# Attention read-out and soft mixture of experts on one core: a ring of 21 buffers of 8 KB per partition in place of 43 of 4 KB

## The chip, the core and the metric

The kernel runs on one core of one Trainium2 chip. What counts is the device time of one execution in microseconds (us). The kernel before took 134.65 us, the median of 3 runs (134.57 to 135.22). The core has five engines with a queue of instructions each: TensorE (PE, with its weight loads listed as PEld), VectorE (DVE), ScalarE (ACT), GpSimd (POOL) and SyncE (SP). Transfers between HBM and the on-chip memory SBUF are issued by an engine's queue (here SP's, and twice ACT's) and carried out by 16 DMA engines. SBUF has 128 partitions; a transfer of a tile moves one row per partition. All data is float32. In sizes, 1 MB is 1,048,576 bytes and 1 KB is 1,024.

## The reference

Eight batches b, eight heads, 512 tokens of width 64 and 32 states per head. First an attention in both directions between tokens and states, then a soft mixture of 8 experts with 4 slots each over all 4608 rows:

```python
scores = scale * x @ state.T;      a  = softmax(scores);   xread = a  @ state
scores2 = scale * state @ x.T;     a2 = softmax(scores2);  sread = a2 @ x
x = concat([xread, sread], tokens)            # (4608, 512)
logits = x @ phi                              # 32 slots
d = softmax(logits, over rows)
slot_input = d.T @ x                          # (32, 512), needs every row
h = relu(slot_input[e] @ w1[e])               # per expert e, w1[e] 512 x 1024
slot_out[e] = h @ w2[e]                       # w2[e] 1024 x 512
out = softmax(logits, over slots) @ slot_out  # (4608, 512)
```

The inputs x and the two weights are 8 MB, 16 MB (w1) and 16 MB (w2). The output is 8.5 MB. No weight can be used before the slot inputs are known, and these need every row of the attention.

## The kernel before, in words

**Stages.** The attention stage runs over the batches; the order of its small steps on all engines is written out in the table `ORDER`, and no scheduler changes it. In it `X.b.g` (L204) transposes a quarter g of batch b on PE, and `R.b.h` (L311) is the last step that reads x of batch b. The stage ends with `SI` (L594), which gives the slot inputs. The h stage (L640) multiplies them with w1: for each half hf of the hidden width and each expert e four column blocks, which together use 1 MB of w1. The so stage (L700) multiplies with w2, for a quarter k of the output width, a half hf and an expert e. `out(k, q)` makes 1 MB of output: eight matmuls into four PSUM tiles (L730), two copies by ACT (L739) and two by DVE (L740) into buffers, and transfers to HBM (L741). `out_st(k)` makes the small output for the state rows, sent in two transfers (L759). The so stage of the next k is interleaved with the outputs of the last.

**The buffer ring.** x, the weights, the outputs and the transposed states `stT_sb` share one pool `big` of `NBIG` = 43 buffers of 4 KB per partition (0.5 MB each). Tiles take the buffers in turn: the n-th tile takes the buffer of the one 43 before it and can be filled once that has been used for the last time. First come `stT_sb` (one buffer) and x (two buffers per batch), then weights are loaded ahead into the 26 buffers that are left. Later loads are issued where the code has freed buffers: two after `R.b.1` (so 16 over the stage), one after the last use of `stT_sb`, and two after each expert of the h stage (`load_w` in `w1_part`). Thus 43 weight buffers are loaded before the first expert of the h stage has been computed; the rest follow as the h stage frees its buffers.

**The queue.** All these transfers stand on SP's queue in program order. The framework gives each transfer one of eight semaphores in rotation (DMAHW0 to DMAHW7 in the listings), and the issue of a transfer waits for the one eight before it to have landed. So at most eight transfers are in flight. An `[waits ...]` in a listing names the semaphores that the instruction waits for: those of DMA, of PE, DVE and ACT (Activation); the number after the underscore has no meaning here.

Of the kernel before, what the change touches and what calls it, by code (L numbers as in the profile page):

```python
# [8 lines left out]
F32 = mybir.dt.float32  # L9
# [6 lines left out]
P = 128  # L16
B = 8
# [7 lines left out]
NBIG = 43  # L25
# [39 lines left out]
def attention_soft_moe(ctx: ExitStack, tc: tile.TileContext, x, stT, phi, w1, w2, out_x, out_s):  # L65
# [14 lines left out]
    stT_sb = big.tile([P, 4, 2, 2, 2, NS], F32, tag="big", name="stT_sb")  # L80
    phi_sb = cp.tile([P, 4, NS], F32, name="phi_sb")
    xb = []
    for b in range(B):
        for k in range(2):
            t = big.tile([P, 2, NJ, 2 * D], F32, tag="big", name=f"x{b}_{k}")
            xv = x[b].rearrange("p (g j c) -> p g j c", g=4, j=NJ)
            if b == 0:
                for g, eng in enumerate((nc.sync, act)):
                    eng.dma_start(t[:, g], xv[:, 2 * k + g])
            else:  # L90
                nc.sync.dma_start(t, xv[:, 2 * k : 2 * k + 2])
            xb.append(t)
# [11 lines left out]
    def load_w2(t, k, e, ft):  # L104
        n = t.shape[1] // P
        t = t.rearrange("p (k f) -> p k f", k=n)
        nc.sync.dma_start(t, w2[e, k, :, ft : ft + n, :])
        for i in range(n):
            w2t[k, e, ft + i] = t[:, i]

    def load_w(n):
        for _ in range(min(n, len(todo))):
            layer, hf, e, k = todo.pop(0)
            t = big.tile([P, F], F32, tag="big", name=f"w{layer}_{hf}_{e}_{k}")
            if layer == 1:
                t = t.rearrange("p (k f) -> p k f", k=2)
                nc.sync.dma_start(t, w1[hf, e, :, 2 * k : 2 * k + 2, :])
                for i in range(2):
                    w1t[hf, e, 2 * k + i] = t[:, i]
            else:  # L120
                load_w2(t, hf, e, k)
# [33 lines left out]
    with ExitStack() as actx:  # L155
# [44 lines left out]
        def X(b, g):  # L200
            r = R[b]
            r[f"xp{g}"] = p = ps_t.tile([P, S], F32, tag="tr", name=f"xt_ps{b}_{g}")
            for j in range(NJ):
                pe.transpose(p[:, P * j : P * j + P], xb[2 * b + g // 2][:, g % 2, j, :], ident)  # L204
# [100 lines left out]
        def R_(b, h):  # L305
# [3 lines left out]
            for j in range(NJ):  # L309
                for g in range(4):  # L310
# [3 lines left out]
                        xb[2 * b + g // 2][:, g % 2, j, D * h : D * h + D],  # L314
# [3 lines left out]
            if h == 1:  # L318
                load_w(2)
# [301 lines left out]
        load_w(NBIG - 2 * B - 1)  # L621
        order = ORDER.split()

        last = max(order.index(f"S.{B - 1}"), order.index("U.1"))
        for i, step in enumerate(order):
# [210 lines left out]
```

## Time and profile before

One profiled execution spans 133.9 us; the runs had a median of 134.65 us, so about 0.75 us lie outside the span.

| What | Value |
|---|---|
| moved by DMA | 51.76 MB (decimal), mean 387 GB/s over the span |
| PE, DVE, ACT, POOL busy | 116.5, 86.0, 79.3, 44.8 us |
| weight transfers | 64 of 512 KB, median 10.0 us from issue to landing |
| output transfers of x rows | 16 of 512 KB, median 5.5 us from issue to landing |
| DMA queue of SP | 14544 packets, 50.93 MB (decimal) |

A row of a table by windows gives the window and its length in us, then the busy time and, in brackets, the instructions of PE, PEld, DVE, ACT and POOL, then the granted clock of PE as a share of full speed, the mean busy share of the 16 DMA engines (which can be a little over 1 because packets overlap) and the GB/s that they moved. A row of a timeline gives the start, the time, the engine (SPq is SP's queue), the line, the operation, output and input, and the count. A row of waits gives who waited for whom, the total in us, how often, and the longest.

### The profile page before, as it was taken

How to read it: one execution, taken by the hardware profiler on the slowest of the kernel's cores; microseconds unless marked ns; L12 is line 12 of the kernel's file. 1: busy time of each engine (PE TensorE's matmuls, PEld its weight loads, DVE VectorE, ACT ScalarE, POOL GpSimd, SP SyncE). 2: the span in 40 equal slices, each digit the busy share in tenths (PEclk: the TensorE clock that was granted, in tenths of full speed). 3: DMA queues.
4: the chain of work that ended last, by engine and by line, in shares of the span. 5: the costliest groups of instructions: out<-in, count | busy, mean ns of one | idle time of the engine just before them, and what ended most of it. 6: DMA issues, size and time to landing. Idle time of an engine off the chain costs nothing.

```text
span 133.9 us, 5045 instructions
## 1 busy us (share of the span) xinstructions
PE 116.5 (87%) x2103; PEld 81.5 (61%) x2103; DVE 86.0 (64%) x216; ACT 79.3 (59%) x195; POOL 44.8 (33%) x64
## 2 busy tenths in 40 slices
PE   0698999999999999999799959999999899999700
PEld 0647676868786867667667636763597449394200
DVE  2009999999999999999995377008940352333610
ACT  3068999999999989888967702210101362535700
POOL 3005383473849066078885247001600000000000
PEclk9999999999999999999999986999999999999995
DMA  3999999999999999999999984999999999998994
GB/s 88 307 391 423 416 415 424 410 421 405 419 415 416 420 413 421 416 419 413 421 410 424 405 345 153 377 399 419 415 420 413 424 410 419 413 418 330 420 415 169
DMA packets 14854, 51.76 MB, mean 387 GB/s; under 512 B 1648, under 2 KB 1904, under 8 KB 14832
## 3 DMA queue, kind: packets, MB, share of 16 engines
q1 hardware_dynamic: 14544, 50.93, 94.8%
q10 hardware_dynamic: 288, 0.52, 1.1%
q8 instruction: 16, 0.26, 0.7%
q14 instruction: 6, 0.05, 0.1%
HBM read 42.53 MB, written 8.91 MB: 384 GB/s over the span
## 4 chain that ended last, share of the span: by engine, by line
PE 45%; DVE 37%; ACT 5%; issue 4%; DMA 3%; DVEq 1%; ACTq 0%
PE h_ps L640 12%; PE so_ps L700 11%; PE o L730 7%; DVE aT L261 6%; DVE l1s L247 6%; DVE q L231 6%; DVE m L236 5%; DVE nm L267 5%; PE xt_ps L204 5%; DMA x<-x_in 3%; DVE r L252 3%; PE sc L218 2%; PE eT_ps L286 2%; PE os L748 2%; ACT out L739 1%
## 5 line engine op out<-in xcount | busy, mean ns | idle before, releaser
L204 PE MATMUL xt_ps<-ident,x 128*128 128x128 f32 x128 | 19.5, 294 | 4.6 <-DMA x<-x_in 4.6
L240 POOL TENSOR_TENSOR q<-q,m 128x512 f32<-128x512 f32 x16 | 16.7, 1049 | 16.7 <-DVE m L236 7.0
L740 DVE COPY out<-o 128x512 f32<-128x512 f32 x16 | 10.3, 686 | 18.7 <-PE o L730 18.7
L209 ACT ACTIVATE xt<-xt_ps 128x512 f32<-128x512 f32 x32 | 18.9, 618 | 5.7 <-PE xt_ps L204 5.6
L204 PEld LDWEIGHTS xt_ps<-ident,x 128*128 128x128 f32 x128 | 15.5, 151 | 7.2 <-issue 5.4
L256 POOL TENSOR_TENSOR q<-q,r 128x512 f32<-128x512 f32 x16 | 16.7, 1048 | 8.0 <-DVE r L252 2.7
L700 PEld LDWEIGHTS so_ps<-w,h_m 128*32 128x32 f32 x512 | 13.8, 110 | 4.2 <-issue 4.1
L640 PE MATMUL h_ps<-w,si_m 128*32 128x512 f32 x128 | 16.0, 650 | 0.4 <-DVE si_m L612 0.4
L700 PE MATMUL so_ps<-w,h_m 128*32 128x128 f32 x512 | 15.6, 274 | 0.8 <-issue 0.8
L231 DVE STREAM_TRANSPOSE q<-sc 128x512 f32<-128x512 f32 x16 | 11.1, 695 | 7.7 <-PE sc L218 7.7
L739 ACT COPY out<-o 128x512 f32<-128x512 f32 x16 | 8.6, 588 | 7.2 <-PE o L730 7.2
L640 PEld LDWEIGHTS h_ps<-w,si_m 128*32 128x32 f32 x128 | 8.7, 118 | 6.3 <-issue 3.6
L272 ACT ACTIVATE e<-sc,nm 128x512 f32<-128x512 f32 x16 | 11.3, 707 | 1.0 <-DVE q L231 0.4
L261 DVE STREAM_TRANSPOSE aT<-q 128x512 f32<-128x512 f32 x16 | 10.8, 687 | 0.2 <-PE eT_ps L286 0.2
L286 PE MATMUL eT_ps<-ident,e 128*128 128x128 f32 x64 | 10.2, 280 | 0.7 <-ACT e L272 0.5
L311 PE MATMUL sr_ps<-x,eT 128*32 128x64 f32 x512 | 10.3, 220 | 0.3 <-ACT eT L294 0.3
L243 ACT ACTIVATE q<-q 128x512 f32<-128x512 f32 x16 | 10.5, 658 | 0.0
L247 DVE TENSOR_REDUCE l1s<-q 128x16 f32<-128x512 f32 x16 | 10.5, 656 | 0.0
L236 DVE TENSOR_REDUCE m<-q 128x16 f32<-128x512 f32 x16 | 10.5, 659 | 0.0
L267 DVE TENSOR_REDUCE nm<-sc 128x1 f32<-128x512 f32 x16 | 10.5, 660 | 0.0
L286 PE MATMUL an_ps<-ident,aT 128*128 128x128 f32 x64 | 9.9, 280 | 0.2 <-DVE aT L261 0.2
L730 PE MATMUL o<-lt_all,so_r 32*128 32x512 f32 x64 | 9.9, 640 | 0.2 <-ACT out L739 0.2
(115 smaller groups left out, 179.3 us busy)
## 6 DMA issues: line engine op xcount, KB each, us to landing
w<-w_in SPq DMA_DIRECT2D x64, 512.0 KB, 10.0
out_x<-out SPq DMA_DIRECT2D x16, 512.0 KB, 5.5
x<-x_in SPq DMA_DIRECT2D x14, 512.0 KB, 9.3
x<-x_in ACTq DMA_DIRECT2D x2, 256.0 KB, 4.7
x<-x_in SPq DMA_DIRECT2D x2, 256.0 KB, 4.3
out_s<-out_s SPq DMA_DIRECT2D x2, 256.0 KB, 5.1
stT_sb<-stT_in SPq DMA_DIRECT2D x1, 384.0 KB, 7.5
stT_sb<-stT_in SPq DMA_DIRECT2D x1, 128.0 KB, 5.6
```

What stands on the lines that cost most here:

```text
L204: pe.transpose(p[:, P * j : P * j + P], xb[2 * b + g // 2][:, g % 2, j, :], ident)
L209: act.mul(r[f"xt{g}"], r[f"xp{g}"], 0.125)
L231: dve.transpose(r[f"q{h}"], r[f"sp{h}"])
L236: dve.tensor_reduce(out=r[f"m1{h}"], in_=r[f"qv{h}"], axis=AX.X, op=ALU.max)
L240: pool.tensor_tensor(v, v, R[b][f"m1{h}"].broadcast_to([P, 16, NS]), op=ALU.subtract)
L247: dve.tensor_reduce(out=l1s[:, i, :, 0:1], in_=R[b][f"qv{h}"], axis=AX.X, op=ALU.add)
L261: dve.transpose(r[f"aT{h}"], r[f"q{h}"])
L267: dve.tensor_reduce(out=r[f"nm2{h}"], in_=r[f"sp{h}"], axis=AX.X, op=ALU.max, negate=True)
L286: pe.transpose(p[:, j, :], r[f"{src}{h}"][:, P * j : P * j + P], ident)
L640: pe.matmul(h_ps[hf][32 * kt : 32 * kt + 32, :], si_m[kt // 2][:, 256 * (kt % 2) + 32 * e : 256 * (kt % 2) + 32 * e + 32], w1t[hf, e, kt], ...
L700: pe.matmul(so[k][32 * i : 32 * i + 32, :], h_m[hf][:, 256 * i + 32 * e : 256 * i + 32 * e + 32], w2t[k, e, 4 * hf + i], start=(hf == 0 an ...
L730: pe.matmul(o[j], so_r[hf][rows, col : col + 128], lt_all[rows, 4 * q : 4 * q + 4, :].rearrange("p b s -> p (b s)"), start=True, stop=True,)
```

## The change

The ring becomes 21 buffers of 8 KB per partition, 1 MB each. `stT_sb` leaves the ring for the pool of constants, so the memory is the same: 43 x 4 KB = 21 x 8 KB + 4 KB = 172 KB per partition. x of a batch is one tile; batches 2 to 7 come in one transfer each, batch 0 in four quarters and batch 1 in two halves as before. A w1 tile holds a whole (hf, e), a w2 tile two experts of a k, for which w2 and the output have another layout in HBM, so that rows of 8 KB are contiguous. An `out(k, q)` is one tile; for k < 3 it is sent in one transfer after all four copies, for k = 3 in two halves as before. There are 46 transfers fewer. The step that loaded into the buffer of `stT_sb` is gone.

```diff
-NBIG = 43
+NBIG = 21
-    stT_sb = big.tile([P, 4, 2, 2, 2, NS], F32, tag="big", name="stT_sb")
+    stT_sb = cp.tile([P, 4, 2, 2, 2, NS], F32, name="stT_sb")
...
+        t = big.tile([P, 4, NJ, 2 * D], F32, tag="big", name=f"x{b}")
+        if b == 0:
+            for g in range(4):
+                (act if g % 2 else nc.sync).dma_start(t[:, g], xv[:, g])
+        elif b == 1:
+            for g in (0, 2):
+                nc.sync.dma_start(t[:, g : g + 2], xv[:, g : g + 2])
+        else:
+            nc.sync.dma_start(t, xv)
...
-    todo = [(1, hf, e, k) for hf in range(2) for e in range(E) for k in range(2)]
-    todo += [(2, k, e, 0) for k in range(4) for e in range(E)]
+    todo = [(1, hf, e) for hf in range(2) for e in range(E)]
+    todo += [(2, k, e) for k in range(4) for e in range(0, E, 2)]
...
+            t = big.tile([P, 2 * F], F32, tag="big", name=f"w{layer}_{k}_{e}")
+            if layer == 1:
+                nc.sync.dma_start(t, w1[k, e])
+            else:
+                nc.sync.dma_start(t, w2[e // 2, k])
...
             if h == 1:
-                load_w(2)
+                load_w(1)
...
-        load_w(NBIG - 2 * B - 1)
+        load_w(NBIG - B)
-            if i == last:
-                load_w(1)
...
-            load_w(2)
+            load_w(1)
...
+            ot = big.tile([P, NJ, 512], F32, tag="big", name=f"out{k}_{q}")
             for jp in range(2):
-                ot = big.tile([P, 2, 512], F32, tag="big", name=f"out{k}_{q}_{jp}")
-                act.copy(ot[:, 0, :], o[2 * jp])
-                dve.tensor_copy(ot[:, 1, :], o[2 * jp + 1])
-                nc.sync.dma_start(out_x[k, q, jp].rearrange("p (i s) -> p i s", i=2), ot)
+                act.copy(ot[:, 2 * jp, :], o[2 * jp])
+                dve.tensor_copy(ot[:, 2 * jp + 1, :], o[2 * jp + 1])
+                if k == 3:
+                    two = slice(2 * jp, 2 * jp + 2)
+                    nc.sync.dma_start(out_x[k, q, :, two], ot[:, two])
+            if k < 3:
+                nc.sync.dma_start(out_x[k, q], ot)
```

Two places on SP's queue show what moves. The first is where loading ahead ends and the h stage begins to free buffers. The names there are w_k_e for w2 of quarter k and expert e, then running numbers; the tile is given as partitions by elements. Before, the loads ahead of the h stage end with w_1_2, the 43rd weight tile; w_1_3 is the first that waits for PE's h stage:

```order
L107 DMA w_0_7_0_1355<-w_in 128x1024 [waits DMAHW4_49,PE_49]
L107 DMA w_1_0_0_1501<-w_in 128x1024 [waits DMAHW5_49,PE_49]
L107 DMA w_1_1_0_1503<-w_in 128x1024 [waits DMAHW6_49,PE_49]
L107 DMA w_1_2_0_1555<-w_in 128x1024 [waits DMAHW7_49,PE_49]
L107 DMA w_1_3_0_1778<-w_in 128x1024 [waits DMAHW0_49,PE_49]
L107 DMA w_1_4_0_1780<-w_in 128x1024 [waits DMAHW1_49,PE_49]
```

In the change each name stands for two experts, and the loads ahead of the h stage end with w_1_0, the 21st weight tile:

```order
L117 DMA w_0_4_1194<-w_in 128x2048 [waits DMAHW1_49,PE_49]
L117 DMA w_0_6_1301<-w_in 128x2048 [waits DMAHW2_49,PE_49]
L117 DMA w_1_0_1447<-w_in 128x2048 [waits DMAHW3_49,PE_49]
L117 DMA w_1_2_1720<-w_in 128x2048 [waits DMAHW4_49,PE_49]
L117 DMA w_1_4_1726<-w_in 128x2048 [waits DMAHW5_49,PE_49]
```

Expert 2 of k = 1, which was among the loads ahead, is now in the first tile that waits for the h stage: 0.5 MB has moved from one side of that point to the other.

The second place is the end of the queue, the outputs of k = 2 and k = 3 (the names out_q_jp before, out_q now):

```order
L759 DMA out_s<-out_s_2099 128x512 [waits DMAHW5_49,Activation_49]
L741 DMA out_x<-out_0_0_2216 128x1024 [waits DMAHW6_49,DVE_49,Activation_49]
L741 DMA out_x<-out_0_1_2220 128x1024 [waits DMAHW7_49,DVE_49,Activation_49]
L741 DMA out_x<-out_1_0_2299 128x1024 [waits DMAHW0_49,DVE_49,Activation_49]
L741 DMA out_x<-out_1_1_2303 128x1024 [waits DMAHW1_49,DVE_49,Activation_49]
L741 DMA out_x<-out_0_0_2322 128x1024 [waits DMAHW2_49,DVE_49,Activation_49]
L741 DMA out_x<-out_0_1_2326 128x1024 [waits DMAHW3_49,DVE_49,Activation_49]
```

The same stretch in the change, where the first row is the small output of the state rows too:

```order
L758 DMA out_s<-out_s_2017 128x512 [waits DMAHW3_49,Activation_49]
L740 DMA out_x<-out_0_2130 128x2048 [waits DMAHW4_49,DVE_49,Activation_49]
L740 DMA out_x<-out_1_2211 128x2048 [waits DMAHW5_49,DVE_49,Activation_49]
L738 DMA out_x<-out_0_2232 128x1024 [waits DMAHW6_49,DVE_49,Activation_49]
L738 DMA out_x<-out_0_2232 128x1024 [waits DMAHW7_49,DVE_49,Activation_49]
```

The two halves of out(2, 1), which could each go once its two copies were made, are one transfer that waits for all four copies; those of k = 3 stay halves.

More of the change, by code (lines that the diff above doesn't have):

```diff
@@ L83, in attention_soft_moe @@
     for b in range(B):
[L84 to L92, printed above, removed]
+        t = big.tile([P, 4, NJ, 2 * D], F32, tag="big", name=f"x{b}")
+        xv = x[b].rearrange("p (g j c) -> p g j c", g=4, j=NJ)
+        if b == 0:
[6 more added lines that the diff above has]
+            nc.sync.dma_start(t, xv)
+        xb.append(t)
         if b == 0:
@@ L100, in attention_soft_moe @@
     w1t, w2t = {}, {}
-    todo = [(1, hf, e, k) for hf in range(2) for e in range(E) for k in range(2)]
-    todo += [(2, k, e, 0) for k in range(4) for e in range(E)]
[L104 to L109, printed above, removed]
+    todo = [(1, hf, e) for hf in range(2) for e in range(E)]
+    todo += [(2, k, e) for k in range(4) for e in range(0, E, 2)]
     def load_w(n):
         for _ in range(min(n, len(todo))):
-            layer, hf, e, k = todo.pop(0)
-            t = big.tile([P, F], F32, tag="big", name=f"w{layer}_{hf}_{e}_{k}")
+            layer, k, e = todo.pop(0)
+            t = big.tile([P, 2 * F], F32, tag="big", name=f"w{layer}_{k}_{e}")
             if layer == 1:
[L116 to L119, printed above, removed]
-            else:
-                load_w2(t, hf, e, k)
+                t = t.rearrange("p (k f) -> p k f", k=4)
+                nc.sync.dma_start(t, w1[k, e])
+                for i in range(4):
+                    w1t[k, e, i] = t[:, i]
+            else:
+                t = t.rearrange("p (e k f) -> p e k f", e=2, k=8)
+                nc.sync.dma_start(t, w2[e // 2, k])
+                for i in range(16):
+                    w2t[k, e + i // 8, i % 8] = t[:, i // 8, i % 8]
     def st_t(b, g):
@@ L203, in X @@
             for j in range(NJ):
-                pe.transpose(p[:, P * j : P * j + P], xb[2 * b + g // 2][:, g % 2, j, :], ident)
+                pe.transpose(p[:, P * j : P * j + P], xb[b][:, g, j, :], ident)
         def xe(b, g):
@@ L313, in R_ @@
                         r[f"eT{h}"][:, j, 32 * g : 32 * g + 32],
-                        xb[2 * b + g // 2][:, g % 2, j, D * h : D * h + D],
+                        xb[b][:, g, j, D * h : D * h + D],
                         start=(j == 0),
@@ L620, in attention_soft_moe @@
         )
-        load_w(NBIG - 2 * B - 1)
+        load_w(NBIG - B)
         order = ORDER.split()
-        last = max(order.index(f"S.{B - 1}"), order.index("U.1"))
-        for i, step in enumerate(order):
+        for step in order:
             name, *args = step.split(".")
             steps[name](*map(int, args))
-            if i == last:
-                load_w(1)
         h_ps = [ps_s.tile([P, 512], F32, tag="sc", name=f"h_ps{i}") for i in range(2)]
@@ L706, in w2_part @@
                 )
-            if hf:
+            if hf and e % 2:
                 load_w(1)
@@ L823 @@
         "w1_in": con(moe_w1.reshape(E, 4, P, 2, 512).transpose(3, 0, 2, 1, 4)),
-        "w2_in": con(moe_w2.reshape(E, 8, P, 4, P).transpose(0, 3, 2, 1, 4)),
+        "w2_in": con(moe_w2.reshape(E // 2, 2, 8, P, 4, P).transpose(0, 4, 3, 1, 2, 5)),
     }
@@ L832 @@
     r = _run(nc, [arrays], core_ids=[0]).results[0]
-    ox = r["out_x"].reshape(4, 2, 2, P, 2, 4, P).transpose(1, 5, 2, 4, 6, 0, 3).reshape(B, S, 512)
+    ox = r["out_x"].reshape(4, 2, P, 2, 2, 4, P).transpose(1, 5, 3, 4, 6, 0, 2).reshape(B, S, 512)
     os_ = r["out_s"].reshape(2, P, 2, B, NS).transpose(3, 4, 0, 2, 1).reshape(B, NS, 512)
```

2 lines of the change are left out of this document (1 added, 1 removed).

## The prediction

> **What bounds the kernel now.** I read the page first, its slices and the table of DMA issues.
>
> ```profile
> GB/s 88 307 391 423 416 415 424 410 421 405 419 415 416 420 413 421 416 419 413 421 410 424 405 345 153 377 399 419 415 420 413 424 410 419 413 418 330 420 415 169
> w<-w_in SPq DMA_DIRECT2D x64, 512.0 KB, 10.0
> ```
>
> A slice is 3.35 us. The DMA engines move about 417 GB/s from the fourth slice on, except in two holes: slices 24 to 26 and slice 37. Eight transfers of 512 KB in flight take 10.0 us at that rate (8 x 524,288 B / 417 GB/s = 10.06 us), so the queue is always full and the issue costs nothing. The table of windows shows the steady part and, in single microseconds, the holes and the end:
>
> ```profile
> 14.00:74.00 60.00, 58.18 (x1187) 43.47 (x1187) 57.28 (x150) 55.63 (x144) 33.67 (x42) 1.00 1.03 417
> 79.00:80.00 1.00, 0.69 (x4) 0.47 (x8) 0.94 (x5) 0.00 (x0) 0.00 (x0) 0.74 0.67 274
> 81.00:82.00 1.00, 1.00 (x10) 0.70 (x6) 0.96 (x2) 0.00 (x0) 1.00 (x1) 0.50 0.15 57
> 82.00:83.00 1.00, 1.00 (x11) 0.72 (x7) 0.96 (x3) 0.63 (x1) 0.71 (x2) 0.55 0.65 160
> ...
> 122.50:122.75 0.25, 0.19 (x1) 0.19 (x2) 0.25 (x2) 0.25 (x2) 0.00 (x0) 1.00 0.45 180
> 123.25:123.50 0.25, 0.25 (x5) 0.25 (x8) 0.01 (x1) 0.21 (x1) 0.00 (x0) 1.00 0.36 147
> 123.50:123.75 0.25, 0.25 (x4) 0.03 (x4) 0.00 (x0) 0.16 (x1) 0.00 (x0) 1.00 0.95 393
> 131.00:132.00 1.00, 0.00 (x0) 0.00 (x0) 0.00 (x0) 0.00 (x0) 0.00 (x0) 0.50 0.80 328
> ```
>
> In the attention stage DVE is the bound (57.28 of 60 us) and the DMA runs behind it, loading ahead. The first hole begins near 79 us, when everything that fits in the ring has landed. The waits of SP's queue from 73 us on name its end, and the timeline gives the moment:
>
> ```profile
> SPq L107 <- PE h_ps L640: 10.4, 6, 7.9
> 81.31 20.20 SPq L107 DMA_DIRECT2D w<-w_in  x21
> ```
>
> At 81.31 us the first expert of the h stage has freed its weights and SP issues again; 21 of the 64 weight transfers are left. From then on two things run side by side. The DMA has 10.5 MB of weights and 8.5 MB of output to move. PE has its own chain, which waits for no weight:
>
> ```profile
> 79.31 10.68 PE h_ps L640 x80
> 90.58 5.29 PE h_ps L640 x48
> 117.20 3.63 PE so_ps L700 x128
> 120.83 1.11 PE o L730 x8
> 121.94 0.57 ACT out L739
> ```
>
> The chain of waits from 79.31 on is almost all PE. The two meet in the second hole: at 122.5 us the DMA share falls to 0.45, to rise again at 123.5. So about half of the engines have run out of work for 1 us, because PE had not made out(2, 1), while the other half is still busy with older transfers until about 123.45. From 123.5 on all are busy until 132. The end is out(2, 1) plus what follows it: 3.25 MB, 3.41e6 B / 417 GB/s = 8.2 us.
>
> **The change part by part.** *Loading ahead.* Before, 43 x 0.5 = 21.5 MB of weights land before the hole; now 21 MB. The point at which loading resumes hangs on PE's first expert and stays at 81.31. So 0.5 MB more is to be moved after it: 524,288 B / 417 GB/s = +1.26 us of DMA work. The DMA stops 1.26 us sooner before the hole, which gives nothing back.
>
> *Issues.* 46 transfers fewer on SP's queue; with a full queue that is 0, and where SP waits for PE (81.31) one issue stands in place of two. If the cover were gone, an issue would cost the 0.33 us of its row below.
>
> *Bytes in flight.* Eight transfers are now 8 MB, and outputs still stand behind the last weights, as they did: 0.
>
> *The whole out(2, 1).* Its halves were issued as their copies ended; now one transfer waits for the last copy:
>
> ```profile
> 122.72 0.33 SPq L741 DMA_DIRECT2D out_x<-out  x1
> ...
> 123.32 0.33 SPq L741 DMA_DIRECT2D out_x<-out  x1
> ```
>
> The first row became data at 123.5, 0.8 us later. Now the issue comes at 123.32 and data at 124.1: +0.60 us for engines that have run dry. The earlier outputs, whole too, find a queue that is behind, so their later issue is covered by it; without this cover each would cost 0.6 us at the most. SP waits longer, but only outputs stand behind it, none of which is ready sooner (out(3, 0) is issued at 125.17).
>
> *The rate with rows of 8 KB.* No transfer here has such rows. The nearest rows are these, the queue of SP from 20 to 60 us (4 KB rows) and that of ACT in the first 14 us (2 KB rows), as packets, MB, share of 16 engines' time:
>
> ```profile
> q1 hardware_dynamic: 4546, 16.55, 101.7%
> ...
> q10 hardware_dynamic: 288, 0.52, 10.8%
> ```
>
> Nine packets are one transfer's part on one engine (eight rows and a completion). With 4 KB rows that part took 1.017 x 40 x 16 / (4546 / 9) = 1.29 us, with 2 KB rows 0.108 x 14 x 16 / 32 = 0.76 us. A straight line through both gives 2.35 us at 8 KB against 2 x 1.29 = 2.58: 9% less, the upper end of a gain, and a far one, since the 2 KB rows ran while the queue was only starting. The lower end is the worst full slice of the page, 405 GB/s against 417, 3% slower. The best full slice is 424, 1.7% faster. I take 1%, between no change and that best slice, since the 4 KB row is nearest. From 81.31 until out(2, 1) the DMA moves 11 MB of weights and 5 MB of output in 8 KB rows, 16.8e6 B or 40.2 us; 1% of it is 0.40 us.
>
> The Trainium skill (DMA: Bandwidth & Descriptors, Why small descriptors are slow) states a fixed overhead of some 3 cycles per packet beside one cycle per 32 B. By that, as an estimate, two rows of 4 KB take 2 x 131 cycles and one of 8 KB 259, 1.1% less, so this term would be 0.46 in place of 0.40; no run here shows it yet.
>
> *x of batch 2.* It was two transfers, now one, and the first transpose of batch 2 needs only the first half. SP's later issues wait for each to land, and PE's row is that transpose:
>
> ```profile
> 12.15 0.33 SPq L91 DMA_DIRECT2D x<-x_in  x1
> 13.39 0.33 SPq L91 DMA_DIRECT2D x<-x_in  x1
> ...
> 13.95 0.66 PE L204 MATMUL xt_ps<-ident,x 128*128 128x128 f32 x4
> ```
>
> The halves had landed at about 12.1 and 13.35; PE comes at 13.95. So the whole has 0.6 us to spare: 0, and each us beyond would be a us of the path, since PE is on it there. Later batches have several us more.
>
> *w2 in pairs.* The last weights were issued near 101 us and land some 10 us later, PE needs them at 117.20; 1 us more and a coarser grain lie in that gap: 0.
>
> *The sum.* The engines that are behind come to out(2, 1) later by 1.26 - 0.40 = 0.86 us; those that run dry by 0.60. The end follows the later: 0.86, less 1% of the one whole output that comes after (2.5 us, 0.03): +0.83 us. The profiled span would be 133.9 + 0.8 = 134.7; the 0.75 us outside it stay, and on the median 134.65 + 0.83 = **135.5 us**.
>
> **The rivals.** *1. The rate rises by 1.7% or more.* Then 1.26 - 0.68 falls below 0.60 and the whole out(2, 1) alone sets the end, +0.60 less what the last whole output gains (1.7% of 2.5 us, 0.04; at 9%, 0.2): +0.4 to +0.56, 135.05 to 135.2 us. For it speaks the straight line above, against it that it rests on the starting queue. The skill's rule (the same page, Rules for kernel authors) is at least 1 MiB per transfer for bandwidth, and its measurement for 16 MB is 425 GB/s, issued from GpSimd; by that, as an estimate 1.9% over the 417 here, it would be this case.
>
> *2. The rate doesn't rise, or falls*, for instance because a row of 8 KB is moved as two packets of 4 KB, so that the change doesn't do what it says there. Then the full 1.26 us remains, 135.9 us; at the worst slice's 3% less, 42.7 us (the same bytes and the last whole output) give 1.3 us more, 137.2 us. For it: nothing in the steady part shows a cost that longer rows would save, since the share is 1.03 throughout.
>
> *3. Not slower: PE's clock.* The rows at 79 to 83 us show a granted clock of 0.74, 0.50 and 0.55, and so ten experts take 10.68 us where the next six take 5.29, which is 0.88 each: 10.68 - 8.82 = 1.86 us lost. If a shifted stage 79 us met the clock otherwise and kept it, PE's chain would be 1.86 us shorter, and the first weights free about 0.9 us sooner. The end by DMA would shift by 1.26 - 0.9 - 0.40 = 0.0, by PE by 0.60 - 1.86 = -1.26: 134.6 us with my rate, down to 133.4 if the rate rises. From 1% more rate on it is faster. Against it: PE's idle time before 79.31, which comes ahead of the low clock, is not touched.
>
> **How the numbers follow.** My forecast, 0.6 to 1.2 us later, has 0.45; rival 1 0.25, rival 2 0.2, rival 3 0.1. A measurement tells 0.5%, 0.67 us, from no change. Slower by more: 0.36 of my own case and all of rival 2, 0.56. Within: 0.09 of my own, rival 1, and 0.03 of rival 3, 0.37. Faster: 0.07 of rival 3. The range of my case is 135.25 to 135.85. For 8 in 10 it reaches into rival 3 down to 134.3 and into rival 2 up to 136.4.
>
> **What would show each step.** The hole should start 1 us or more before 79 and end at the same 82 us; SP's first issue in the h stage should stay at 81.3. Windows from 20 to 70 us show the rate: 421 GB/s fits mine, 424 and more rival 1, 417 or less rival 2, and packets of 8 KB should be half as many. The hole at 122.5 should be gone, or lie with all engines from 123 to 124.1. The issue of out(2, 1) should be at 123.3. PE's chain from 79.3 to 126 should be as it is; a different length there, or a PE that waits for x at 14 us, would make the prediction wrong.

## The result and the profile after

The changed kernel takes 137.23 us (median of 4 runs, 136.87 to 137.67) against 134.89 us (4 runs, 134.57 to 135.22): the ratio is 1.0148, with a 95% interval of 1.0109 to 1.0186. By this ratio it is 2.0 us slower (the two medians lie 2.3 us apart), where 0.83 us was forecast.

The page of the changed kernel (its slices, its packets, its largest group of DMA issues) and, for the packets, the page of the kernel before:

```profile
GB/s 90 304 399 430 437 420 430 417 425 410 430 425 422 425 425 427 420 425 422 425 427 425 309 29 285 273 408 432 417 434 422 427 420 425 417 423 330 407 413 117
DMA packets 8518, 51.76 MB, mean 381 GB/s; under 512 B 944, under 2 KB 1200, under 8 KB 2864
...
w<-w_in SPq DMA_DIRECT2D x32, 1024.0 KB, 19.5
```

```profile
DMA packets 14854, 51.76 MB, mean 387 GB/s; under 512 B 1648, under 2 KB 1904, under 8 KB 14832
```

The change does what it says: 14832 packets under 8 KB have become 2864, so a row of 8 KB is one packet, and from the fourth slice up to the first hole the rate is higher than before. But the first hole is deeper (309, 29, 285, 273 where it was 405, 345, 153, 377), and the second, slice 37, is still there. The windows of the kernel before that the prediction did not show, and then those of the changed kernel (columns: window and length, then busy time and instructions of PE, PEld, DVE, ACT and POOL, then PE's clock, the share of the DMA engines, GB/s):

```profile
74.00:82.00 8.00, 6.28 (x95) 4.38 (x99) 4.95 (x15) 2.21 (x7) 3.25 (x5) 0.84 0.77 307
82.00:90.00 8.00, 8.00 (x72) 5.43 (x65) 0.99 (x3) 2.20 (x4) 1.64 (x3) 0.94 0.96 355
85.00:86.00 1.00, 1.00 (x16) 0.79 (x12) 0.00 (x0) 0.00 (x0) 0.00 (x0) 1.00 1.00 352
90.00:122.00 32.00, 30.97 (x627) 19.84 (x628) 14.04 (x33) 8.35 (x21) 2.71 (x3) 1.00 1.03 416
132.00:133.00 1.00, 0.00 (x0) 0.00 (x0) 0.00 (x0) 0.00 (x0) 0.00 (x0) 0.50 0.07 29
```

```profile
14.00:74.00 60.00, 58.02 (x1182) 43.55 (x1178) 57.12 (x149) 55.40 (x143) 33.75 (x42) 1.00 1.01 424
74.00:82.00 8.00, 6.28 (x100) 4.75 (x101) 4.89 (x17) 2.52 (x8) 2.95 (x5) 0.91 0.44 182
81.00:82.00 1.00, 1.00 (x9) 0.84 (x5) 0.97 (x3) 0.00 (x0) 0.73 (x1) 0.50 0.00 0
82.00:90.00 8.00, 8.00 (x69) 6.78 (x60) 1.30 (x3) 2.21 (x4) 1.94 (x3) 0.87 0.93 325
85.00:86.00 1.00, 1.00 (x15) 0.95 (x10) 0.00 (x0) 0.00 (x0) 0.00 (x0) 1.00 1.05 238
86.00:87.00 1.00, 1.00 (x14) 0.93 (x10) 0.00 (x0) 0.00 (x0) 0.00 (x0) 1.00 0.67 213
90.00:122.00 32.00, 30.93 (x630) 19.77 (x626) 14.02 (x32) 8.28 (x20) 2.71 (x3) 1.00 1.01 422
...
123.75:124.00 0.25, 0.25 (x4) 0.21 (x8) 0.00 (x0) 0.25 (x1) 0.00 (x0) 1.00 0.62 262
124.25:124.50 0.25, 0.25 (x8) 0.14 (x1) 0.00 (x0) 0.00 (x0) 0.00 (x0) 1.00 0.62 262
124.50:124.75 0.25, 0.25 (x5) 0.12 (x1) 0.00 (x0) 0.00 (x0) 0.00 (x0) 1.00 0.32 131
...
132.00:133.00 1.00, 0.00 (x0) 0.00 (x0) 0.00 (x0) 0.00 (x0) 0.00 (x0) 0.50 1.02 422
133.00:134.00 1.00, 0.00 (x0) 0.00 (x0) 0.00 (x0) 0.00 (x0) 0.00 (x0) 0.50 0.32 127
```

The steady rate rises from 417 to 424 GB/s. In the hole the engines now run wholly dry (share 0.00 at 81 us, where it was 0.15). In the 8 us after it they move 325 GB/s in place of 355, and from 85 to 86 us a share of 1.05 carries only 238 GB/s: the engines count as busy, and yet the packets of that moment take far longer. Later they are faster again, 422 against 416, and at the end they are busy until about 133.3, where before they were done soon after 132.

These rows add up. Rate times length gives the bytes moved in each window (the rates are rounded, which leaves some 0.1 us open):

| window | before | changed | difference, KB (1000 B) | at 424 GB/s |
|---|---|---|---|---|
| 14 to 82 us | 27476 | 26896 | -580 | 1.37 us behind |
| 82 to 90 us | 2840 | 2600 | -240 | 0.57 us behind |
| 90 to 122 us | 13312 | 13504 | +192 | 0.45 us ahead |
| together, 14 to 122 us | | | -628 | 1.5 us behind |

The spans differ by 135.8 - 133.9 = 1.9 us, which is 0.4 us more than these bytes explain. The 580 KB at 82 us are, but for some 60, the 0.5 MB (524 KB) that no longer fit. The 420 KB by which the changed kernel is ahead at 74 us (7 GB/s for 60 us) are worth nothing: the ring is full sooner and the hole begins sooner.

The bytes are a mean over the DMA engines, and the end is set by the one that is furthest behind. That one is seen where a transfer lands, since a transfer has landed when its last part has. These rows are the issue of out(2, 0) (in the kernel before, of its second half) with its time to landing, and the same for the last output, first of the kernel before and then of the change:

```profile
118.62 0.44 SPq L741 DMA_DIRECT2D out_x<-out  x1
DMA to landing us min/median/max: 6.3/6.3/6.3
128.16 0.64 SPq L741 DMA_DIRECT2D out_x<-out  x1
DMA to landing us min/median/max: 4.8/4.8/4.8
```

```profile
119.06 0.33 SPq L740 DMA_DIRECT2D out_x<-out  x1
DMA to landing us min/median/max: 7.6/7.6/7.6
129.58 0.77 SPq L738 DMA_DIRECT2D out_x<-out  x1
DMA to landing us min/median/max: 5.1/5.1/5.1
```

Before, out(2, 0) has landed at 124.9 us and the last output at 133.0; in the change at 126.6 and 134.7. So the change is 1.7 us behind at out(2, 0), and from there both kernels need the same 8.0 to 8.1 us. A trace records sixteen landings of each transfer, read here as one for each DMA engine: those of out(2, 0) lie between 122.7 and 124.9 us before, between 123.6 and 126.6 in the change. The foremost engine is 0.9 us later, the hindmost 1.7. So the changed kernel has lost nearly all of its 1.9 us by out(2, 0), and its later hole costs next to nothing.

The timeline of the changed kernel, at the places that the prediction named:

```profile
13.97 0.66 PE L202 MATMUL xt_ps<-ident,x 128*128 128x128 f32 x4
...
79.61 10.76 PE L635 MATMUL h_ps<-w,si_m 128*32 128x512 f32 x80 [0.35 <-DVE si_m L610]
81.20 9.53 SPq L117 DMA_DIRECT2D w<-w_in  x10
...
124.13 0.33 SPq L740 DMA_DIRECT2D out_x<-out  x1
```

PE does not wait for x of batch 2 (13.97, before 13.95), its chain in the h stage is 0.3 us later (79.61 against 79.31), SP's loads start again when they did (81.20 against 81.31), and out(2, 1) is issued 0.8 us later than its second half was (123.32).

### The profile page after: what moved, and what is told of

Same layout as the page of the kernel before. It is cut to its first block, busy times and chain, and to the rows that moved or that the text cites. A ratio compares the mean times of both kernels' runs of the same rounds, so it can differ in the third digit from the quotient of the medians.

```text
span 135.8 us, 4954 instructions
## 1 busy us (share of the span) xinstructions
PE 116.9 (86%) x2103; PEld 83.2 (61%) x2103; DVE 86.1 (63%) x216; ACT 79.3 (58%) x195; POOL 44.9 (33%) x64
## 2 busy tenths in 40 slices
DMA packets 8518, 51.76 MB, mean 381 GB/s; under 512 B 944, under 2 KB 1200, under 8 KB 2864
## 4 chain that ended last, share of the span: by engine, by line
DVE 41%; PE 39%; ACT 6%; issue 4%; DMA 3%; DVEq 1%; ACTq 0%
PE h_ps L635 12%; PE so_ps L695 11%; DVE l1s L245 7%; PE o L725 7%; DVE q L229 6%; DVE aT L259 6%; DVE nm L265 6%; DVE m L234 5%; PE xt_ps L202 3%; DVE r L250 3%; DMA x<-x_in 3%; PE os L747 2%; DVE r L249 1%; PE sc L216 1%; ACT xt L207 1%
## 5 line engine op out<-in xcount | busy, mean ns | idle before, releaser
L635 PEld LDWEIGHTS h_ps<-w,si_m 128*32 128x32 f32 x128 | 10.4, 118 | 4.6 <-issue 3.2
```

The source lines that it names most:

```text
L635: pe.matmul(h_ps[hf][32 * kt : 32 * kt + 32, :], si_m[kt // 2][:, 256 * (kt % 2) + 32 * e : 256 * (kt % 2) + 32 * e + 32], w1t[hf, e, kt], ...
```

## The experiments

Theory A: the bytes that are left for the DMA engines after the hole set the end; 0.5 MB less ahead costs 1.26 us, and the rest of the change hardly counts. Theory B: the whole out(2, 1), issued late, sets the end. Theory C: large transfers with long rows start worse after the hole. Theories D, E and F came later: D, the layout of w2 in memory; E, buffers that come free 1 MB at a time; F, a half-filled buffer in my own kernels. Ratios are to the kernel before on the same chip, with 95% intervals. Its median there lay between 135.04 and 135.32 us, so 0.1% is 0.135 us.

### The outputs: e1, e5, e7

e1 is the change with all outputs in halves. e7 is the kernel before, in which for k < 3 both halves are issued only after the last copy, the second half first; it is the prediction's term for out(2, 1) alone.

```diff
 (e1, e5)
-                if k == 3:
-                    two = slice(2 * jp, 2 * jp + 2)
-                    nc.sync.dma_start(out_x[k, q, :, two], ot[:, two])
-            if k < 3:
-                nc.sync.dma_start(out_x[k, q], ot)
+                two = slice(2 * jp, 2 * jp + 2)
+                nc.sync.dma_start(out_x[k, q, :, two], ot[:, two])
 (e7)
-                nc.sync.dma_start(out_x[k, q, jp].rearrange("p (i s) -> p i s", i=2), ot)
+                late.append((jp, ot))
+                if k < 3 and jp == 0:
+                    continue
+                for i, t in late[::-1]:
+                    nc.sync.dma_start(out_x[k, q, i].rearrange("p (i s) -> p i s", i=2), t)
+                late = []
```

> The change as it is, but every out(k, q) is sent in two halves as before, each when its own two copies are made. Measured so far: 134.9 us before, 137.2 us with the change. In the change's profile out(2, 1) is issued at 124.13 us (before: first half 122.72) and all engines are busy again at 124.9 (before: 123.5). Theory A (work left on the DMA engines since the restart in the h stage sets the end; 0.5 MB more of it, and a worse start): about half of the engines are busy until 124.5 anyway, so this gives 0 to 0.3 us, 136.9 to 137.2. Theory B (the late whole output sets the end): the first half goes 0.6 to 1.0 us sooner and so does the end, 136.2 to 136.6.

> The kernel before with its rows of 4 KB and 43 buffers, but for the first three of the four output blocks of each half both 0.5 MB stores are issued only after the last of the four copies. Theory B (the late whole output leaves engines dry near 123 us, which is the prediction's term): +0.60 us, ratio 1.004. Theory A (half of the engines still have loads queued there and end last anyway): +0.2 us at most, ratio 0.999 to 1.002. Nothing else differs from before, so 14 to 74 us stays at 417 GB/s and the hole before the h stage stays where it was.

e1: 137.7 us, 1.015 (1.0099 to 1.0201), no better than the change. e7: 135.22 us, 0.9982 (0.9945 to 1.002), so the 0.60 us (0.44%) lie outside the interval. The windows of e7 show that the late issue did make a hole, a deeper one than before, from 123 us on:

```profile
123.00:124.00 1.00, 1.00 (x10) 0.39 (x9) 0.40 (x1) 0.69 (x3) 0.00 (x0) 1.00 0.50 201
124.00:125.00 1.00, 0.94 (x10) 0.29 (x2) 0.43 (x1) 0.47 (x1) 0.00 (x0) 1.00 0.79 324
```

The share says that half of the engines' time is idle there, and the median does not move. Theory B falls. The landings say why: in all profiles but those of e8 and e9 (18 in number), whether out(2, 1) goes whole or in halves, early or late, the last output lands 8.0 to 8.2 us after out(2, 0). The engine that is furthest behind still has work of out(2, 0) when out(2, 1) is issued; in e7 that work lands at 125.3 us. e5, the kernel e3 below with all outputs in halves, says the same with the 0.5 MB given back:

> The change with the 0.5 MB loaded ahead again (as in the kernel e3_cap_back, ratio 1.0091) and, beside it, every output stored in halves of 0.5 MB as before the change. Theory A (bytes left for the DMA engines after the restart set the end, and the form of the stores does not matter): the same as e3_cap_back, ratio 1.009 (1.006 to 1.012), about 136.2 us against 135.0. Theory B in its weak form (a whole output decides only once the backlog of 0.5 MB is gone): up to the 0.60 us of the prediction's term for out(2,1) below that, ratio 1.004 to 1.006. Theory C (large loads with long rows restart badly after the hole): ratio 1.009, and 82 to 90 us at 325 to 345 GB/s, as in the change and in e3_cap_back, against 355 before.

e5: 137.0 us, 1.010 (1.0058 to 1.0143), where e3 has 1.0091.

### The 0.5 MB: e2, e3

e2 is the kernel before with one buffer less; e3 is the change with the 0.5 MB given back: once its last reader is through, half a w2 tile is loaded into the memory of `stT_sb`.

```diff
 (e2)
-NBIG = 43
+NBIG = 42
 (e3)
-    stT_sb = cp.tile([P, 4, 2, 2, 2, NS], F32, name="stT_sb")
+    stT_sb = st4.tile([P, 4, 2, 2, 2, NS], F32, tag="st4", name="stT_sb")
...
+                if (k, e) == (1, 2):
+                    nc.sync.dma_start(t[:, 1], w2[e // 2, k, :, 1])
...
+    def load_half():
+        t = st4.tile([P, 8, P], F32, tag="st4", name="w2_half")
+        nc.sync.dma_start(t, w2[1, 1, :, 0])
```

> The kernel before with one buffer of 4 KB less (42), so that 21 MB of weights are loaded ahead, as in the change; rows, transfers and outputs as before. Theory A: 0.5 MB more after the restart, at 417 GB/s 1.26 us, on engines that never run dry: 136.1 us. Theory B: the engines that run dry at 122.5 us have 1 us to spare, so at most 0.3 us: 135.2 us. Theory C (the worse restart with transfers of 1 MB is the main loss): near 134.9 to 135.5, with 355 GB/s from 82 to 90 us as before.

> The change, but the buffer of the transposed states takes half a weight tile after its last use, so that 21.5 MB are loaded ahead again; the first transfer after the restart is then 0.5 MB. Outputs whole. Theory A: 0.5 MB less after the restart, at 424 GB/s 1.24 us: 136.0 us. Theory B: out(2, 1) is as late as in the change: 137.0 to 137.2. Theory C: the bad restart stays, 325 GB/s from 82 to 90 us, and so do at least 0.6 of the 2.3 us.

e2: 136.8 us, 1.0101 (1.0054 to 1.0148), 1.36 us for 0.5 MB, where 1.26 was the price. Its windows show hardly any other loss:

```profile
14.00:74.00 60.00, 57.99 (x1182) 43.34 (x1185) 57.20 (x150) 55.52 (x144) 33.69 (x42) 1.00 1.03 417
74.00:82.00 8.00, 6.28 (x95) 4.62 (x99) 4.91 (x15) 2.25 (x7) 3.23 (x5) 0.85 0.61 243
82.00:90.00 8.00, 8.00 (x72) 6.06 (x64) 1.02 (x3) 2.21 (x4) 1.66 (x3) 0.94 0.97 360
90.00:122.00 32.00, 31.06 (x628) 19.93 (x628) 14.06 (x33) 8.37 (x21) 2.72 (x3) 1.00 1.03 413
```

It is 512 KB behind at 82 us, starts again as before does (360 GB/s), and loses some 100 KB more from 90 to 122 us (413 GB/s in place of 416). e3: 136.65 us, 1.0091 (1.0062 to 1.012). That seemed to leave 0.9% of the loss unexplained and sent me after theories C, D and E; it was an error of this kernel, as F shows below.

### Rows, layout and buffers: e4, e6, e9, e10, e11

All of these read 4 KB rows. e4 is the change with its loads in 0.5 MB. e6 is e3 with its weights so. e9 is the kernel before with w2 in the layout of the change, so that a transfer takes 4 KB out of each row of 8 KB. e10 is the kernel before, issuing the second load of each pair first, so that SP waits until 1 MB is free. e11 is e6 with x, w2 and outputs in memory and in transfers as before; only the 1 MB buffers remain.

```diff
 (e4, e6)
-                nc.sync.dma_start(t, w2[e // 2, k])
+                for i in range(2):
+                    nc.sync.dma_start(t[:, i], w2[e // 2, k, :, i])
 (e9)
-        nc.sync.dma_start(t, w2[e, k, :, ft : ft + n, :])
+        nc.sync.dma_start(t, w2[e // 2, k, :, e % 2, ft : ft + n, :])
 (e10)
+        for t, src in put[::-1] if n == 2 else put:
+            nc.sync.dma_start(t, src)
 (e11, beside e6)
-                nc.sync.dma_start(t[:, i], w2[e // 2, k, :, i])
+                nc.sync.dma_start(t[:, i], w2[e + i, k])
...
-            if k < 3:
-                nc.sync.dma_start(out_x[k, q], ot)
+                nc.sync.dma_start(out_x[k, q, jp].rearrange("p (i s) -> p i s", i=2), ot[:, 2 * jp : 2 * jp + 2])
```

> The change, but each weight tile and each x of batches 2 to 7 comes in two transfers of 0.5 MB with rows of 4 KB into the same 8 KB buffer; outputs whole. Steady rate 417 in place of 424 GB/s. Theory A without a restart effect: the rate costs 11 MB at 1.7%, 0.46 us: 137.7. Theory C (long rows or large transfers make the restart worse by 0.6 us): the windows from 82 to 90 us return from 325 to 355 GB/s, and the sum is 137.1. Theory B: 137.2, no change.

> The change with the 0.5 MB loaded ahead again, and each buffer of 1 MB filled by two transfers of 0.5 MB with rows of 4 KB (x and the outputs stay as in the change). Theory C (the rest of the loss, 0.9 % in e3_cap_back, is the restart with large transfers and long rows): the first windows after the hole come back to before's 355 GB/s, the steady rate falls from 424 to 417 (0.4 us by 16.8 MB less 1.7 %), and the net is a ratio of 1.000 to 1.006. Theory A with rate alone: what is loaded ahead is as before, the rate is as before, so nothing but the whole outputs is left: ratio 1.000 to 1.004. If the coarse buffer itself (1 MB is freed at a time, so loads begin later and in pairs after the hole) is what costs, neither comes back: ratio 1.009 to 1.015, with 82 to 90 us below 340 GB/s in spite of the short rows.

> The kernel before with its 43 buffers of 4 KB and transfers of 0.5 MB, but with w2 laid out in memory as the change has it: the rows of 4 KB that one transfer reads stand 8 KB apart, not one behind the other. Theory D (the layout of w2 in memory makes the transfers after the hole slower; e6_cap_rows4k reads w2 so too, and is at 1.0154): ratio 1.005 to 1.012, with 82 to 90 us below 340 GB/s against 355. Theory E (what costs is that memory is freed and filled 1 MB at a time): no effect of the layout, ratio 0.998 to 1.002 and 82 to 90 us at 338 to 360 GB/s, as in the three kernels with buffers of 4 KB so far.

> The kernel before with everything as it is, but of the two 0.5 MB loads that belong together the second is issued first, so that SP waits until both buffers are free (1 MB at a time). Theory E in the form that the wait for a whole MB costs at the restart: the first loads after the hole are issued 0.42 us later (81.73 in place of 81.31), ratio 1.003 to 1.008. Theory D, or a cost of the buffers that is not in the time at which they come free: ratio 0.998 to 1.002.

> Only the buffers of the change: 21 of 8 KB, with the 0.5 MB loaded ahead again beside them, while every transfer is 0.5 MB with rows of 4 KB and x, w2 and the outputs lie in memory as before. Theory E (buffers of 1 MB): as e6_cap_rows4k, ratio 1.010 to 1.018, 82 to 90 us below 340 GB/s, and an end of the transfers that is spread over more than 2 us. Theory D (layout of w2) or the whole stores of e6_cap_rows4k: ratio 0.998 to 1.004.

| kernel | median, us | ratio | interval |
|---|---|---|---|
| e4, the change with 4 KB rows | 137.54 | 1.0158 | 1.0106 to 1.0209 |
| e6, e3 with 4 KB rows | 137.49 | 1.0154 | 1.01 to 1.0208 |
| e9, before with w2 strided | 136.27 | 1.0076 | 1.0043 to 1.0109 |
| e10, before waiting in pairs | 135.16 | 1.001 | 0.9982 to 1.0039 |
| e11, only the buffers | 136.53 | 1.0085 | 1.0048 to 1.0122 |

With w2 laid out so that 4 KB are taken out of rows of 8 KB, the kernel before is 0.76% slower (e9; none of its windows is used here), which none of my theories had at the start; waiting for 1 MB costs nothing that can be told (e10). e4 and e6 pay the strided reads, so they do not tell what rows of 8 KB are worth. e11 looked like a proof of theory E. But its windows show where it lost:

```profile
82.00:90.00 8.00, 8.00 (x71) 6.29 (x64) 0.89 (x3) 2.15 (x4) 1.62 (x2) 0.94 0.88 302
84.00:85.00 1.00, 1.00 (x15) 0.90 (x11) 0.00 (x0) 0.28 (x1) 0.00 (x0) 1.00 0.68 143
```

Engines run dry a second time, at 84 us. e3, e5, e6 and e11 put the odd 0.5 MB in the middle of a pair: the first 1 MB buffer that came free after the hole received only the other half, and the next load waited for the next buffer, until 83.1 us in e11. For e3 itself the cost of this does not show in its span: its profile is of its fastest execution, 135.48 us against a median of 136.65.

### The ring filled whole: e13, e14, e15

e13 is e11, and e14 is e3, with the pairs shifted: the odd 0.5 MB is the last one loaded ahead, and each buffer after the hole but the very last gets 1 MB. In e14 w2 lies in memory in the order of loading, since its pairs are others. e15 is e4 with w2 in memory as before.

```diff
 (e13, e14)
-    todo += [(2, k, e) for k in range(4) for e in range(0, E, 2)]
+    todo += [(2, f, min(f + 2, 32)) for f in (*range(0, 10, 2), *range(11, 32, 2))]
 (e15)
-                    nc.sync.dma_start(t[:, i], w2[e // 2, k, :, i])
+                    nc.sync.dma_start(t[:, i], w2[e + i, k])
```

> As e11_grain (21 buffers of 8 KB and one of 4 KB, transfers of 0.5 MB with rows of 4 KB, x, w2 and outputs in memory as before), but the odd 0.5 MB is the last one loaded ahead, so that every buffer of 1 MB is filled with 1 MB from the first transfer after the hole on; in e11_grain the first of them got only 0.5 MB, and the next pair waited until 83.1 us. Theory F (the 0.85 % of e11_grain are that late half MB): ratio 0.998 to 1.003, and no dip of the DMA engines at 84 to 85 us. Theory E (buffers of 1 MB cost by themselves): 1.006 to 1.012 as before.

> The change with the same 0.5 MB ahead again and every buffer filled whole: transfers of 1 MB with rows of 8 KB for all weights but two halves, x and outputs as in the change. Theory F and theory A: nothing is left of the loss but the steady rate's gain of 1.7 % after the hole (20 MB at 424 in place of 417 GB/s, 0.8 us): ratio 0.993 to 0.999, which would beat the kernel before. Theory E or theory C (rows of 8 KB restart worse, slow packets at 85 to 87 us): 1.003 to 1.010, as e3_cap_back with 1.0091.

> As e4_rows4k (the change's 21 buffers and so 0.5 MB less ahead, every load in transfers of 0.5 MB with rows of 4 KB, ratio 1.0158), but w2 lies in memory as before, each 0.5 MB in one piece. Theory A (0.5 MB less ahead is 1.26 us, measured 1.0101 with buffers of 4 KB) with theory D (the layout of w2 was 0.76 % of e4_rows4k): ratio 1.007 to 1.011. Theory E (buffers of 1 MB cost 0.85 % beside the 0.5 MB): 1.015 to 1.020.

e13: 135.49 us, 1.0025 (0.9996 to 1.0054). e14: 135.37 us, 0.9995 (0.9966 to 1.0024). e15: 136.5 us, 1.0087 (1.0053 to 1.0121). Theory F holds: from e11 to e13, which differ in nothing else, 0.6% goes away (0.5 either way), and from e3 to e14, where the order of w2 in memory differs too, 0.96% (0.4). With the ring filled whole, buffers of 1 MB cost at most 0.5% (e13), and 1 MB transfers of 8 KB rows together with whole outputs neither cost nor gain what can be told (e14). e15 pays 0.87% for its 0.5 MB, and against e4 it gains 0.7% by the layout, as e9 said. The windows of e14 and then of e15:

```profile
14.00:74.00 60.00, 58.33 (x1232) 43.96 (x1222) 57.48 (x149) 55.78 (x145) 34.45 (x42) 1.00 1.01 424
74.00:82.00 8.00, 6.28 (x106) 4.85 (x108) 4.93 (x17) 2.73 (x8) 2.75 (x5) 1.00 0.60 246
82.00:90.00 8.00, 8.00 (x77) 6.32 (x72) 1.97 (x5) 2.21 (x4) 2.15 (x3) 1.00 0.96 383
90.00:122.00 32.00, 30.73 (x626) 19.66 (x614) 14.65 (x34) 9.46 (x23) 2.71 (x3) 1.00 1.01 417
```

```profile
14.00:74.00 60.00, 58.09 (x1194) 43.50 (x1193) 57.03 (x151) 55.69 (x146) 33.57 (x42) 1.00 1.03 416
74.00:82.00 8.00, 6.39 (x83) 5.03 (x87) 5.38 (x16) 2.18 (x6) 3.44 (x6) 0.83 0.67 256
82.00:90.00 8.00, 8.00 (x72) 6.61 (x63) 0.52 (x2) 1.78 (x4) 1.45 (x2) 0.95 0.97 371
90.00:122.00 32.00, 30.90 (x626) 19.64 (x624) 14.48 (x33) 8.79 (x22) 2.71 (x3) 1.00 1.02 419
```

Both start again after the hole at 371 to 383 GB/s, not at the change's 325. Counted as above, e14 is 68 KB behind at 82 us, gains 224 KB by 90 and 32 KB by 122 us: 0.45 us ahead, and its span is 0.3 us shorter. e15 is 468 KB behind, then gains 128 and 96: 0.6 us behind, and its span is 0.7 us longer. e2 is 568 KB behind at 122 us, 1.3 us, and its span is 1.2 us longer. In these three the bytes at 122 us tell the end within 0.2 us. In others they don't: e6 ends some 0.5 us later and e17 some 0.5 us sooner than its bytes say. So the 0.4 us that the change has over are no sign of a loss of their own.

### The order of w2 in memory: e16, e17

The change loads blocks that lie 4 MB apart one after the other, the kernel before blocks 2 MB apart, e14 neighbours. e16 is the change, e17 the kernel before, with w2's blocks in the order of loading.

```diff
 (e16)
-                nc.sync.dma_start(t, w2[e // 2, k])
+                nc.sync.dma_start(t, w2[k, e // 2])
...
-        "w2_in": con(moe_w2.reshape(E // 2, 2, 8, P, 4, P).transpose(0, 4, 3, 1, 2, 5)),
+        "w2_in": con(moe_w2.reshape(E // 2, 2, 8, P, 4, P).transpose(4, 0, 3, 1, 2, 5)),
 (e17)
-        nc.sync.dma_start(t, w2[e, k, :, ft : ft + n, :])
+        nc.sync.dma_start(t, w2[k, e, :, ft : ft + n, :])
```

> The change, with nothing altered but the order in which the blocks of 1 MB of w2 lie in memory: one behind the other in the order in which they are loaded, where the change loads blocks that lie 4 MB apart. Theory D (blocks 4 MB apart make the transfers slow that run beside each other after the hole): ratio 1.007 to 1.010, which is what 0.5 MB less ahead costs alone (1.0087 in e15_rows4k_flat), and 82 to 90 us at 365 GB/s or more, as against 325. If it is the rows of 8 KB instead, or the transfers of 1 MB: ratio 1.012 to 1.018 and below 350 GB/s there.

> The kernel before, with nothing altered but the order in which the blocks of 0.5 MB of w2 lie in memory: one behind the other as they are loaded, where before loads blocks that lie 2 MB apart. Theory D, if 2 MB apart costs too: 82 to 90 us above 355 GB/s, ratio 0.993 to 0.998. If only blocks 4 MB apart cost: ratio 0.998 to 1.002.

e16: 137.16 us, 1.0122 (1.0073 to 1.0171). e17: 135.43 us, 1.0018 (0.9987 to 1.0048). The order is worth nothing in the kernel before. In the change the ratio lies at the lower end of the second expectation, and its interval reaches over both; the windows of e16 answer to the second, since the restart is as bad as in the change:

```profile
82.00:90.00 8.00, 8.00 (x72) 4.56 (x64) 1.19 (x3) 2.21 (x4) 1.82 (x3) 0.94 0.84 316
86.00:87.00 1.00, 1.00 (x16) 0.68 (x12) 0.00 (x0) 0.00 (x0) 0.00 (x0) 1.00 0.80 213
```

The order of the blocks is not shown to be the cause.

### PE's clock: e8, e12, e18

Six (e8) or twelve (e12) transposes, of which nothing is read, stand ahead of the h stage of the kernel before; e18 is e14 with six.

```diff
+        def warm():
+            p = ps_t.tile([P, 4, P], F32, tag="tr", name="warm_ps")
+            for i in range(6):
+                pe.transpose(p[:, i % 4, :], ident, ident)
 (e12, beside e8)
-            for i in range(6):
+            for i in range(12):
```

> The kernel before with six more 128x128 transposes on PE, of which nothing is read, after the last transposes ahead of the h stage, so that PE has no idle stretch just before 79 us. If PE's granted clock falls at 79 to 83 us (.74 .50 .50 .55 there) because of the low use of PE at 77 to 79 us, it stays up in more of the runs: the chain of the h stage starts up to 1.86 us earlier in those, buffers come free earlier, ratio 0.990 to 0.997. If the clock falls for another reason, the six transposes only add about 0.4 us of PE time ahead of the h stage or lie beside other waits: ratio 1.000 to 1.003.

> The kernel before with twelve more 128x128 transposes on PE ahead of the h stage, of which nothing is read (six gave 0.9963). If they keep PE's granted clock at 1.0 through 79 to 83 us (.74 .50 .50 .55 before), the h stage ends up to 1.86 us earlier and the loads behind it start earlier by as much: ratio 0.990 to 0.997. If the engines' work after the restart sets the end whatever PE does, the h stage moves and the end does not: 0.998 to 1.002, since the first load after the hole waits only for the first matmuls of the h stage.

> The kernel e14_odd_rows8 (rows of 8 KB, all buffers in use, w2 in the order of loading; 0.9995) with the six transposes of e8_warm (0.9963 with the kernel before) ahead of the h stage. If the gain of the six transposes is real and independent: ratio 0.993 to 0.998. If it was the spread of the runs, as twelve transposes with 0.9997 suggest: 0.998 to 1.002.

e8: 134.99 us, 0.9963 (0.9934 to 0.9993). e12: 135.08 us, 0.9997 (0.9972 to 1.0023). e18: 135.22 us, 0.9996 (0.9966 to 1.0025). A window and a row of the timeline of e12:

```profile
81.00:82.00 1.00, 1.00 (x14) 0.92 (x10) 0.96 (x3) 0.00 (x0) 0.16 (x1) 1.00 0.07 29
```

```profile
80.18 9.06 PE L645 MATMUL h_ps<-w,si_m 128*32 128x512 f32 x80 [0.35 <-DVE si_m L617]
```

There the clock stayed at 1.00 where it was 0.50, the ten experts took 9.06 us in place of 10.68, and PE was through with them 0.75 us earlier (89.24 against 89.99). The kernel was no faster. That the transposes kept the clock is not shown. e10 and e17 have none of them and the attention stage of before, and their profiles show 1.00 from 79 to 83 us and 9.06 us as well. So the clock falls in some executions and not in others, and the median of the kernel before holds both kinds. Of the 114 executions of that kernel listed beside these runs, the 54 with a mean clock of 0.98 or more took 134.97 us in the median, the other 60 took 135.47 us; the mean also counts PE's idle end, so this is a hint and no price. e8 alone is below 1 by its interval, and neither relative confirms it, so I do not call it a gain. No kernel tried here beats the one before beyond doubt; the 1 MB version to keep would be e14, which ties with it.

## Why the prediction was wrong, point by point

**What bounds the kernel.** Right: the DMA engines' work after the hole sets the end. out(2, 1) made late (e7) changes nothing that can be told, and 0.5 MB more of that work (e2) costs what its bytes cost.

**Loading ahead, +1.26 us.** Right as a price: e2 measured 1.36 us, e15 1.18 us, and the changed kernel is 1.37 us behind at 82 us. That the engines stop sooner before the hole "gives nothing back" was right too. e14 shows the same from the other side: with the 0.5 MB given back and the ring filled whole, the whole loss is gone. The terms put at nothing held as well: PE does not wait for x of batch 2, and no stage of PE waits for w2.

**The rate, -0.40 us.** In size right for the long stretch, and in part by luck: from 90 to 122 us the change gains 192 KB, 0.45 us. The steady rate itself rose as rival 1 had it, by 1.7% (417 to 424), not by the 1% that I chose, nor by the 9% of the straight line; but only some 32 us of the 40 ran at it. An estimate from the overhead per packet that the Trainium skill states (DMA: Bandwidth & Descriptors, Why small descriptors are slow) was 1.1%. The trace, 1.7%, is above it. As time, the gain shows in no median: e14 has the better rate and only ties, and the change is 0.6% (0.5 either way) slower than e15, which lacks the same 0.5 MB and has rows of 4 KB.

**The whole out(2, 1), +0.60 us.** Wrong. It was issued later than I said (124.13, of which 0.44 us after the last copy ended I cannot explain), the half-dry hole moved to 123.75 to 125, and none of it counts (e1, e7). The sum gave the engines that run dry and those that are behind the later of two ends. The engines that had run dry had room enough: they are not the ones that end last. The prediction let the others be through with their older work at about 123.45 us; the last part of out(2, 0) landed at 124.9, so that these could not have used out(2, 1) sooner.

**The sum, +0.83 us: the step that failed.** It brought the engines that are behind to out(2, 1) later by 1.26 - 0.40 = 0.86 us, all of them alike, as if they went back to their steady rate once SP issued again. The row of before already said otherwise: 355 GB/s from 82 to 90 us against 416 later. In the changed kernel this restart is at 325, a loss of 0.57 us that the sum put at nothing. It falls unevenly on the engines. At out(2, 0) the foremost engine is 0.9 us later, as forecast, and the hindmost, which sets the end, 1.7. That gap opens at the restart: the landings of the fourth MB after the hole are 3.1 us apart in the change, those of the same MB before 0.9. The 1.7 us, 0.1 from there to the last landing and 0.2 from that to the end of the span make up the 1.9 us of the spans. Neither the restart nor the uneven engines stood in the prediction, nor a rival that had them: rival 1 had the rate and so expected 0.4 to 0.56 us, rival 2 had the loss without the rate. Rival 2's 135.9 to 137.2 us held the median nearly, for a wrong reason.

**Rival 3, PE's clock.** It did not happen in the change's profile, where the clock is as low as before (0.50 at 81 to 82 us), and the change is slower. What a kept clock is worth stays open, as said under e12.

**The median and the span.** I took 0.75 us as the time outside the span, by setting the span of one execution against the median of others. In the runs listed with both, the time outside is 1.8 us on average for every kernel, so the profiled execution of before took some 135.7 us, 0.4 to 0.8 us above the medians of that kernel. The difference of the two spans is sound only because the changed kernel's profile is also its slowest run, 0.44 us above its median.

**What stays open.** e14 and the change differ by 1.53% (0.48 either way, the two intervals added in squares), while 0.5 MB cost 1.01% in e2 and 0.87% in e15. What the change loses beyond the 0.5 MB is 0.6% (0.5 either way) against e15, and 0.5% (0.6) against e2, which is not clear of nothing. The profiles put it into the restart: 325, 299 and 316 GB/s in the change, e1 and e16, against 371 in e15 and 383 in e14. Each of these is a single execution, and the gap between the engines differs: in e16 the foremost engine is 1.5 us later than before at out(2, 0) and the hindmost 1.3. The rows suggest that engines which have run wholly dry for longer start worse with rows of 8 KB, but e14 has such rows too, and ran dry for a shorter time. A hole of the same length without the lack of 0.5 MB was not tried.

Nor is PE's low clock at the restart told apart from it: with rows of 8 KB and every buffer filled whole, the three slow restarts have it and the two fast ones (e14 with 383, e18 with 386) do not. With the clock at 0.50, PE frees the next buffer later, so SP's second load is issued at 82.91 us in the change and at 82.04 in e14. Against the clock as the cause speaks that the first load lands only from 85.1 us on, so the second was there in time, and that with rows of 4 KB the kept clock goes with no clear gain: 355 GB/s before, 352 in e12, 358 in e17.

## What to carry to other kernels

Where loads run ahead of a stage into a ring that fills, price the ring's bytes first: each that no longer fits is moved later, at full price (here 0.5 MB, 1.2 to 1.4 us), while a better rate ahead of the full ring gains nothing and behind it at most its per cent. The DMA engines do not run level, and the end is that of the hindmost; a mean share or rate, and a forecast made from it, can miss this. Larger transfers with longer rows are worth taking only if the ring's capacity stays whole, to the last odd half buffer, and even then they only tied here. An experiment that gives one cost back has to be read in its own trace before its remainder is explained: the half-filled buffer of e3 and e11 cost 0.6 to 0.9% and looked like a property of the hardware.

## What the runs showed of the hardware

- After the engines have run dry, or nearly, they do not return to their rate at once: 355 GB/s over the next 8 us in the kernel before, 299 to 325 in the change and its nearest relatives. In part they stand still, in part packets are slow: a share of 1.05 with 238 GB/s from 85 to 86 us, where the steady state has 1.01 with 424. In the kernel before, the same microsecond shows 352 GB/s with a share of 1.00.
- Reading 4 KB out of each row of 8 KB in HBM cost 0.76% of the kernel (e9), and undoing it gained 0.7% (e4 to e15), with packets of the same size and number. Whether it is the stride of 8 KB or the 4 MB between the blocks is open.
- The sixteen landings of one transfer do not come together: those of out(2, 0) lie 2.2 us apart before and 3.0 in the change. In 18 profiles the last output landed 8.0 to 8.2 us after the last part of out(2, 0).
- Half of the DMA engines' time can be idle for a microsecond near the end (e7, share 0.50 from 123 to 124 us) at no cost in the median, since others end last.
- PE's granted clock can fall in one execution and not in another behind the same stage: 0.50 at 81 to 82 us before, 1.00 in e10 and e17, where ten experts took 9.06 us in place of 10.68.
